# A planner's cost table: a longer way from the late loads to their use, and no delay between dependent passes on TensorE

## The chip, the cores and the metric

The kernel runs on one core of one Trainium2 chip. The metric is the device time of one execution in microseconds (us), median of several runs. Engines are named as in the profile: PE is TensorE (PEld its weight loads), DVE is VectorE, ACT is ScalarE, POOL is GpSimd, SP is SyncE, which issues nearly all DMAs.

## The reference, cut to what matters

Three layers follow each other: an attention over packed queries, a soft mixture of experts, and a feed-forward layer with a softmax gate and a norm. All inputs and the output are fp32.

```python
# attention: batch 8, heads 8, seq 576, head_dim 64, 32 packed queries p
p_packed = sm_attn(p, k, v); out = sm_attn(q, p_packed, p_packed)
# soft MoE: x (4608, 512), phi (512, 32), w1 (8, 512, 1024), w2 (8, 1024, 512), 4 slots an expert
logits = x @ phi
d = softmax(logits, axis=0); slot_input = d.T @ x
for e in range(8):
    slot_out[e] = maximum(slot_input[e] @ w1[e], 0) @ w2[e]
x = softmax(logits, axis=1) @ slot_out
# SoLU layer: w_in (512, 1024), w_out (1024, 512)
h = x @ w_in; solu = h * softmax(h)
out = ((solu - mean) / sqrt(var + 1e-6) * g_ln) @ w_out      # (4608, 512)
```

## The kernel before

The work has three phases. **Phase 1** is the attention and the logits, for four units `u` of two batches `b` each. The steps are named by their builders: `mk_A1` (scores of the packed queries against k), `mk_TR` (transposes), `mk_A4` (times v), `mk_BD`, `mk_B` (scores of q), `mk_S` (five groups `g` of transposes and a softmax a unit), `mk_A2T`, `mk_slots`. A(7) stands below for the step `mk_A` of batch 7, S(4,3) for group 4 of unit 3, the last step of `mk_S`. Phase 1 ends in `SIT`, the slots' input. **Phase 2** streams the experts' weights past `SIT`: `mk_w1` and `mk_w2` for experts 0 to 3, `mk_w1` for experts 4 to 7, and then the second weights of experts 4 to 7 (the late experts) in four column blocks k = 0 to 3 (`mk_block`), so that a block's result is ready for the next layer before the following block has arrived. When a block k is complete, ACT copies it (`so`, L1124), PE transposes it with a small matmul (`tr`, L1128), ACT writes it into `SO` (L1055), and PE multiplies it with the first weight of the last layer (`sw_pe`, L1330: two halves n of 512 columns for each block c; written sw(c,n) here). After sw(3,0) and sw(3,1), ACT and DVE write the two halves of `swr` (L1338, L1342). **Phase 3** needs `swr` for its first matmul (`h`, L1394) and then runs 36 tiles of 128 rows, bounded by the matmuls of L1533 and L1539.

The weights come as 256 *granules* of 128 KB, nine to a load `("w", i)` of 1152 KB. Load i is called w`i`. Granules 192 to 255 are those of the four blocks, 16 granules a block, four for each late expert; they lie in the loads w21 to w28. Load w27 is cut in three (1, 4 and 4 granules), and w28 has the last 4. One granule is 4 matmul records in the trace (two matmuls, each in two passes of fp32). SP issues all loads in one fixed order from one queue, each as soon as a buffer is free: 14 in `ring`, three more (`ring2`) for w5, w6 and w7, which lie over memory of phase 1. Of these, w6 waits for the last matmul of S(4,3), L556.

The order on every engine is made by a planner (`Plan`) when the kernel is built: each step is an `op` with a price in ns, its dependencies, and the buffers it takes and gives back; the delay from a step to one that depends on it comes from a table (`LAT`, 30 ns from PE to PE), from the step's own `lat` (2200 ns after a load) or from a pair `(step, delay)`. The planner walks through time, takes on each engine the ready step with the longest way to the end, repeats that 250 times with random changes to these ways, and keeps the order whose weighted goals come first (the last sw step 1.0, `SIT` 0.3, the last `wlo` 0.1). Where PE would idle in phase 1, a matmul on zeros fills it (L380), in one fixed place of the order. The planner also counts PE's matmuls, and prices the arrival of its next block of code:

```python
plan.blocks = (97, 126, 80, 3800, 45000)
plan.goals = [(x, 1.0), (o_SIT, 0.3), (o_lo, 0.1)]
```

The first block ends at matmul 97, each later one 126 further; a block is asked for 80 matmuls ahead and taken to need 3800 ns.

Of the kernel before, what the change touches and what calls it, by code (L numbers as in the profile page):

```python
# [179 lines left out]
def pack_attention__soft_moe__solu_kernel(  # L180
# [16 lines left out]
    NE = 8  # L197
# [21 lines left out]
    NS1, NS2, NS3 = 122, 125, 142  # L219
    NL = 4  # L220
    LATE = 32 * NE - 16 * NL
# [19 lines left out]
    with ExitStack() as p12, tc.manual_schedule():  # L241
# [18 lines left out]
        def op(*args, urgent=0, **kw):  # L260
            return plan.op(*args, urgent=urgent, rank=now[0], **kw)
# [30 lines left out]
        loaded, ld, W = {}, {}, {}  # L292

        def load(key, part):
            def go():
                if part == 0:
                    pool = W["ring2"] if key in RING2 else ring
                    loaded[key] = pool.tile([128, RW], FP32, tag="r", name="r")
                t = loaded[key]
                if key[0] in "kq":  # L300
                    c0, c1 = (1152 * c for c in halves(key)[part:part + 2])
                    nc.sync.dma_start(out=t[:, c0:c1], in_=(kT if key[0] == "k" else qT)[key[1]][:, c0:c1])
                elif key[0] == "v":
                    nc.sync.dma_start(out=t, in_=v[key[1], key[2]])
                elif key[0] == "w":
                    c0, c1 = (256 * c for c in cuts(key[1])[part:part + 2])
                    nc.sync.dma_start(out=t[:, c0:c1], in_=w12[key[1]][:, c0:c1])
                else:
                    src = (w_out if key[0] == "wo" else w_in)[key[1]].bitcast(UINT32)
                    nc.sync.dma_start(out=t[:, :2048].bitcast(UINT32), in_=src)  # L310

            return go
# [13 lines left out]
        def ring_of(key):  # L326
            return "ring2" if key in RING2 else "ring"

        o_pl = [p_load(0, 2)]
        for key in order:  # L330
            if key[0] in "kq":
                c = halves(key)
                ld[key] = [
                    op("DMA", 1425 * (c[n + 1] - c[n]), load(key, n), acq=[] if n else ["ring"], lat=2200)
                    for n in range(len(c) - 1)
                ]
            elif key[0] == "w":
                c = cuts(key[1])
                for part in range(len(c) - 1):
                    x = op("DMA", 317 * (c[part + 1] - c[part]), load(key, part), acq=[] if part else [ring_of(key)], lat=2200)  # L340
                    for j in range(c[part], c[part + 1]):
                        ld["g", 9 * key[1] + j] = x
            else:
                ns = 2540 if key[0] in ("wo", "wi") else 2850
                ld[key] = op("DMA", ns, load(key, 0), acq=[ring_of(key)], lat=2200)
            if key == ("v", 0, 0):
                o_pl.append(p_load(2, NB))
# [583 lines left out]
        y = op("DVE", 150, f0, [o_M[NU - 1], o_e], acq=["A2T"], rel=["A2T"])  # L931
        x = op("PE", 110, f1, [o_M[NU - 1], y], acq=["w"], pairs=1)
        x = op("DVE", 460, f2, [x, o_e], rel=["w"])
        x = op("PE", 110, f3, [x], acq=["w"], pairs=2)
        x = op("DVE", 70, f4, [x], rel=["w"])
        x = op("ACT", 190, f5, [x])
        x = op("DVE", 70, f6, [x, o_S[NU - 1]])
        x = op("PE", 110, f7, [x], acq=["w"], pairs=2)
        x = op("DVE", 736, f8, [x], rel=["w"])
        x = op("PE", 860, f9, [x, o_SI[NU - 1]], acq=["w"], pairs=8)  # L940
        x = o_SIT = op("DVE", 200, f10, [x], rel=["w"])
# [37 lines left out]
        o_hT, o_SOT, o_w1, o_w2, o_r2 = {}, {}, {}, {}, []  # L979
# [13 lines left out]
        def stream(g0, g1, pe, ns, deps, acq, rel):  # L993
            i = g0
            while i < g1:
                j = i + 1
                while j < g1 and ld["g", j] == ld["g", i]:
                    j += 1
                done = [ring_of(("w", i // 9))] if j % 9 == 0 or j == 32 * NE else []
                deps = [op("PE", ns * (j - i), pe(i, j), [ld["g", i]] + deps, acq=acq if i == g0 else [],  # L1000
                           rel=done + (rel if j == g1 else []))]
                if done == ["ring2"]:
                    o_r2.extend(deps)
                i = j
            return deps[0]

        def hz_zero():
            nc.gpsimd.memset(W["hz"], 0.0)
# [91 lines left out]
        def mk_block(k, e, dep):  # L1100
            s0 = LATE + 4 * (NL * k + e - NE + NL)

            def pe(g0, g1):
                def go():
                    if g0 == s0 and start:
                        ps_t["b", k] = bank()
                    for i in range(g0, g1):
                        for c in range(2):
                            q, r = divmod(i - s0, 2)
                            f = 2 * (i - s0) + c  # L1110
                            g, j = divmod(f, 2)
                            a = 2 * r + c
                            nc.tensor.matmul(
                                out=ps_t["b", k][32 * a:32 * a + 32, 0:128],
                                lhsT=hT_t[e][:, j, g, :],
                                rhs=gran(i)[:, 128 * c:128 * c + 128],
                                start=(start and q == 0),
                                stop=(end and q == 1),
                            )
                return go  # L1120

            def act():
                so_t["b", k] = W["k"].tile([128, 128], FP32, tag="so", name="so", bufs=3)
                nc.scalar.copy(so_t["b", k], ps_t.pop(("b", k))[:, 0:128])  # L1124

            def tr():
                ps_t["bt", k] = bank()
                nc.tensor.matmul(  # L1128
                    out=ps_t["bt", k][:, 0:4 * NL], lhsT=so_t["b", k], rhs=e4[:, 4 * (NE - NL):4 * NE], start=True, stop=True
                )  # L1130

            def act2():
                so_out(4 * (NE - NL), 4 * NE, k, k + 1, ps_t.pop(("bt", k))[:, None, 0:4 * NL])

            start, end = e == NE - NL, e == NE - 1
            y = stream(s0, s0 + 4, pe, NS3, [dep, o_hT[e], o_w2[NE - NL - 1]], ["w"] if start else [], [])
            if end:
                x = op("ACT", 200, act, [y], rel=["w"])
                x = op("PE", 165, tr, [x], acq=["w"])
                o_SOT["k", k] = op("ACT", 230, act2, [x], rel=["w"], urgent=10 ** 5)  # L1140
            return y
# [5 lines left out]
        x = None  # L1147
        for k in range(4):
            for e in range(NE - NL, NE):
                x = mk_block(k, e, x)  # L1150
# [13 lines left out]
        x = op("ACT", 1200, c_hi, [o_2], urgent=10 ** 5)  # L1164
        x = op("DVE", 1300, c_lo, [x], urgent=10 ** 5)
# [85 lines left out]
        o_wo, o_wi, o_bd = [], [], []  # L1251
# [47 lines left out]
        x = op("ACT", 480, sc_act, [o_bd[-1]], rel=["v"])  # L1299
        for f in (sc_dve, sc_dve2, sc_dve3, sc_dve4):  # L1300
            x = op("DVE", 430, f, [x], acq=["u"] if f is sc_dve2 else [])
        for k in range(8):
# [11 lines left out]
            y = op("DVE", 1300, q1, [x, o_wo[k]])  # L1314
            y = op("Pool", 700, q2, [y, o_3])
# [8 lines left out]
        def sw_pe(cs, ns):  # L1324
            def go():
                for n in ns:
                    if not cs[0]:
                        sw_t.append(W["ps"].tile([96, 512], FP32, tag="sw", name="sw"))
                    for c in cs:
                        nc.tensor.matmul(  # L1330
                            out=sw_t[n], lhsT=W["SO"][:, c].rearrange("p r s -> p (r s)"),
                            rhs=wif[:, c, 512 * n:512 * n + 512], start=(c == 0), stop=(c == 3),
                        )
            return go

        def mk_sw(n, dep):
            def act():
                nc.scalar.copy(W["sw"][n], sw_t[n])  # L1338

            def dve():  # L1340
                dst = W["sw"][n][64:96, :]
                nc.vector.tensor_tensor(out=dst, in0=sw_t[n][64:96], in1=dst.bitcast(FP32), op=ALU.subtract)  # L1342

            x = op("PE", 980, sw_pe((3,), (n,)), [dep, *o_SOT.values()])
            y = op("ACT", 478, act, [x], urgent=10 ** 6)
            op("DVE", 602, dve, [y], urgent=10 ** 6)
            return x

        x = None
        for c in range(3):  # L1350
            for n in range(2):
                x = op("PE", 980, sw_pe((c,), (n,)), [x, *o_wi, o_SOT["k", c]] + [o_SOT[e] for e in range(NE - NL)])
        x = mk_sw(0, x)
        x = mk_sw(1, x)
        plan.blocks = (97, 126, 80, 3800, 45000)
# [9 lines left out]
    with ExitStack() as p3, tc.manual_schedule():  # L1365
# [7 lines left out]
        op = plan.op  # L1373
# [326 lines left out]
```

## Time and profile before

| | us |
|---|---|
| median of 3 runs (lowest to highest) | 400.67 (400.15 to 402.09) |
| the profiled execution | 399.89 |
| its span, first to last instruction | 398.1 |
| phases 1 and 2, to the start of the first `h` | 182.0 |
| phase 3 | 216.1 |

The span is what the views below divide; the execution's own time has 1.8 us more around it. The profile gives busy time by engine, a strip of 40 slices, the chain of work that ended last, and for each wait which engine or DMA ended it.

### The profile page before, as it was taken

The numbers are of one execution on the slowest core, as the hardware profiler recorded it, in microseconds if no ns is written. First come the engines' busy times: TensorE is split into PE (matmuls) and PEld (weight loads), VectorE is DVE, ScalarE is ACT, GpSimd is POOL, SyncE is SP. The second block draws the span as 40 slices with busy tenths as digits, with TensorE's granted clock in tenths as the row PEclk, the third lists the DMA queues.
The fourth block names the chain that finished last, engine by engine and source line by source line (L and its number), as shares of the span: only waits on it lengthen the run. The fifth ranks groups of instructions, "written<-read, shape, count | busy, mean of one in ns | idle before, by whom it ended". The sixth has DMA issues, their size and how long they took to land.

```text
span 398.1 us, 9638 instructions
## 1 busy us (share of the span) xinstructions
PE 377.1 (95%) x3772; PEld 196.9 (49%) x3772; DVE 276.2 (69%) x562; ACT 231.3 (58%) x434; POOL 208.8 (52%) x311
## 2 busy tenths in 40 slices
PE   8889999988989998898999999999999999999996
PEld 3445566555535673543444444444444444444445
DVE  2169799888977838937977676676766776667621
ACT  1447797859544834105976665666556566755620
POOL 1033346334233572694878656556675666566630
PEclk9999999999999999999999999999999999999999
DMA  8999999999999999950267685677656655775771
GB/s 309 420 420 421 413 419 418 416 418 416 390 400 418 412 418 420 418 212 1 53 156 172 130 152 118 135 146 159 143 121 134 155 136 129 137 158 132 119 170 56
DMA packets 89421, 99.26 MB, mean 249 GB/s; under 512 B 75936, under 2 KB 76576, under 8 KB 82080
## 3 DMA queue, kind: packets, MB, share of 16 engines
q1 hardware_dynamic: 89088, 98.58, 75.9%
q8 instruction: 29, 0.48, 0.5%
q14 instruction: 16, 0.13, 0.1%
q10 hardware_dynamic: 288, 0.07, 0.1%
HBM read 70.85 MB, written 9.44 MB: 202 GB/s over the span
## 4 chain that ended last, share of the span: by engine, by line
PE 71%; DMA 15%; DVE 6%; ACT 3%; issue 2%; SPq 1%; POOL 0%; ACTq 0%; DVEq 0%; POOLq 0%
PE o L1533 29%; PE o L1539 14%; DMA r<-kT 6%; DMA r<-w 5%; PE h L1394 4%; PE sc L396 3%; PE w L1020 3%; DMA r<-qT 3%; PE w L1071 2%; PE w L556 2%; PE w L479 2%; PE sw L1330 2%; PE o L1546 1%; DVE s3t L1424 1%; PE w L670 1%
## 5 line engine op out<-in xcount | busy, mean ns | idle before, releaser
L1533 PE MATMUL o<-whi,th 128*128 128x512 f16 x280 | 106.2, 379 | 0.9 <-DMA th<-hi 0.9
L1533 PE MATMUL o<-wlo,th 128*128 128x512 f16 x280 | 106.1, 379 | 0.0
L1503 POOL TENSOR_TENSOR lo<-x,hi 128x1024 f16<-128x1024 f32 (+1 forms) x37 | 77.3, 2092 | 30.2 <-ACT hi L1481 28.5
L1533 PEld LDWEIGHTS <-th 128*128 128x128 f16 x560 | 54.6, 98 | 67.0 <-DMA th<-hi 1.4
L1539 PE MATMUL o<-whi,tl 128*128 128x512 f16 x280 | 66.5, 380 | 0.0
L1443 ACT ACTIVATE e<-s3t,nv 128x1024 f32<-128x1024 f32 x36 | 41.3, 1149 | 39.7 <-DVE nmean L1437 39.5
L1481 ACT ACTIVATE hi<-s3t,nr,rs 128x1024 f16<-128x1024 f32 x35 | 43.4, 1239 | 23.0 <-POOL nr L1464 22.8
L1424 DVE SCALAR_TENSOR_TENSOR s3t<-h,e 128x1024 f32<-128x1024 f32 (+1 forms) x37 | 44.0, 1190 | 17.3 <-ACT e L1415 17.2
L1402 DVE TENSOR_REDUCE nm<-h 128x1 f32<-128x1024 f32 (+1 forms) x37 | 44.0, 1191 | 14.0 <-PE h L1394 13.8
L1473 DVE TENSOR_SCALAR x<-s3t,nmean,rs 128x1024 f32<-128x1024 f32 x35 | 28.8, 824 | 23.1 <-POOL rs L1460 23.0
L1415 ACT ACTIVATE e<-h,nm 128x1024 f32<-128x1024 f32 (+1 forms) x37 | 39.9, 1079 | 7.5 <-DVE nm L1402 5.1
L1539 PEld LDWEIGHTS <-tl 128*128 128x128 f16 x280 | 24.9, 98 | 34.3 <-issue 8.6
L1394 PE MATMUL h<-swr,cT 96*128 96x512 f32 x72 | 28.9, 484 | 1.2 <-DVE swr L1342 0.9
L1561 DVE TENSOR_TENSOR ob<-o,winv 128x512 f32<-128x512 f32 x35 | 23.9, 684 | 7.2 <-PE o L1539 7.2
L380 PE MATMUL w<-wz 128*128 128x512 f16 x92 | 26.1, 379 | 0.8 <-DVE A L575 0.4
L600 POOL TENSOR_TENSOR A<-A,bsum 128x512 f32<-128x512 f32 (+1 forms) x18 | 18.1, 1020 | 15.8 <-DVE bsum L596 10.6
L1020 PE MATMUL w<-r,SIT 128*32 128x256 f32 x256 | 21.9, 384 | 0.0
L1460 POOL TENSOR_TENSOR rs<-rs,half 128x1 f32<-128x1 f32 x36 | 20.1, 558 | 2.9
L1459 POOL TENSOR_TENSOR rs<-V,w 128x1 f32<-128x1 f32 x36 | 7.4, 207 | 25.3 <-ACT e L1443 25.2
L454 POOL TENSOR_SCALAR r<-s 128x1 f32<-128x1 f32 x16 | 4.2, 265 | 30.2 <-ACT a L421 29.4
L421 ACT ACTIVATE a<-sc,nb 128x576 f32<-128x576 f32 x16 | 11.8, 739 | 13.6 <-DVE nb L416 13.5
L416 DVE TENSOR_REDUCE nb<-sc 128x1 f32<-128x576 f32 x16 | 11.5, 747 | 11.7 <-PE sc L396 11.7
(203 smaller groups left out, 635.6 us busy)
## 6 DMA issues: line engine op xcount, KB each, us to landing
r<-w SPq DMA_DIRECT2D x27, 1152.0 KB, 15.7
r<-v SPq DMA_DIRECT2D x8, 1152.0 KB, 21.5
r<-kT SPq DMA_DIRECT2D x7, 1152.0 KB, 22.0
r<-qT SPq DMA_DIRECT2D x7, 1152.0 KB, 22.2
out<-ob SPq DMA_DIRECT2D x31, 256.0 KB, 2.3
r<-w_in SPq DMA_DIRECT2D x4, 1024.0 KB, 22.0
r<-w_out SPq DMA_DIRECT2D x4, 1024.0 KB, 21.8
r<-w SPq DMA_DIRECT2D x3, 512.0 KB, 16.9
```

Of the source, the lines that this page charges most:

```text
L380: nc.tensor.matmul(out=t[:, 0:FN], lhsT=wz[:, 0:128], rhs=wz[:, 0:FN], start=True, stop=True)
L1020: nc.tensor.matmul(out=hp[32 * g:32 * g + 32, 0:256], lhsT=SIT[:, k, :], rhs=gran(i), start=(k == 0), stop=(k == 3),)
L1394: nc.tensor.matmul(out=w, lhsT=cT[:, t, :], rhs=swr[n], start=True, stop=True)
L1402: nc.vector.tensor_reduce(out=z["nm"][:, h:h + 1], in_=hcols(h), axis=AX.X, op=ALU.max, negate=True)
L1415: nc.scalar.activation(out=z["e"][:, cols(h)], in_=hcols(h), func=ACTF.Exp, bias=z["nm"][:, 0:1], accum_out=z["S"][:, h:h + 1],)
L1424: nc.vector.scalar_tensor_tensor(out=z["s"][:, cols(h)], in0=hcols(h), scalar=1.0, in1=z["e"][:, cols(h)], op0=ALU.mult, op1=ALU.mult, acc ...
L1443: nc.scalar.activation(out=z["e"], in_=z["s"], func=ACTF.Square, bias=z["nv"], scale=2.0 ** -15, accum_out=z["V"])
L1473: nc.vector.tensor_scalar(out=z["x"][:, cols(h)], in0=z["s"][:, cols(h)], scalar1=z["n"], scalar2=z["r"], op0=ALU.add, op1=ALU.mult,)
L1481: nc.scalar.activation(out=z["hi"][:, cols(h)], in_=z["s"][:, cols(h)], func=ACTF.Identity, scale=z["r"], bias=z["nr"])
L1503: nc.gpsimd.tensor_tensor(out=z["lo"][:, cols(h)], in0=z["x"][:, cols(h)], in1=z["hi"][:, cols(h)], op=ALU.subtract)
L1533: nc.tensor.matmul(out=z["o"], lhsT=z["th"][:, c, :], rhs=w[:, c, :], start=(c == 0 and w is whi), stop=False)
L1539: nc.tensor.matmul(out=z["o"], lhsT=z["tl"][:, c, :], rhs=whi[:, c, :], start=False, stop=(c == 7))
```

## The change

Three places of the planner's cost table change. A load w14 or later counts 2900 ns from its end to its first use, where it was 2200. Within a late expert's column blocks (granules from 192), a PE step that follows another of the same chain counts no delay, where it was 30 ns. The same holds between the sw steps. No operation, buffer, size or dependency changes; the planner's search runs again on the new prices.

```diff
-                    x = op("DMA", 317 * (c[part + 1] - c[part]), load(key, part), acq=[] if part else [ring_of(key)], lat=2200)
+                    x = op("DMA", 317 * (c[part + 1] - c[part]), load(key, part), acq=[] if part else [ring_of(key)],
+                           lat=2900 if key[1] >= 14 else 2200)
...
-                deps = [op("PE", ns * (j - i), pe(i, j), [ld["g", i]] + deps, acq=acq if i == g0 else [],
-                           rel=done + (rel if j == g1 else []))]
+                x = op("PE", ns * (j - i), pe(i, j), [ld["g", i]] + deps, acq=acq if i == g0 else [],
+                       rel=done + (rel if j == g1 else []))
+                deps = [(x, 0) if g0 >= LATE else x]
...
-            y = stream(s0, s0 + 4, pe, NS3, [dep, o_hT[e], o_w2[NE - NL - 1]], ["w"] if start else [], [])
+            y = stream(s0, s0 + 4, pe, NS3, [dep and (dep, 0), o_hT[e], o_w2[NE - NL - 1]], ["w"] if start else [], [])
...
-            x = op("PE", 980, sw_pe((3,), (n,)), [dep, *o_SOT.values()])
+            x = op("PE", 980, sw_pe((3,), (n,)), [(dep, 0), *o_SOT.values()])
...
-                x = op("PE", 980, sw_pe((c,), (n,)), [x, *o_wi, o_SOT["k", c]] + [o_SOT[e] for e in range(NE - NL)])
+                x = op("PE", 980, sw_pe((c,), (n,)), [x and (x, 0), *o_wi, o_SOT["k", c]] + [o_SOT[e] for e in range(NE - NL)])
```

The plan of phase 3 is word for word the same. SP's loads and stores stand in the same order. In phases 1 and 2 PE keeps its 214 steps, and 111 of them stand elsewhere, by up to 11 places; the zero fills that are emitted in phase 1 go from 92 to 82. Lines after 340 move by one, after 1000 by two.

PE, the end of phase 2, from the load w26 to the last sw step, before. `r_2900` is w26, `r_2945` w27, `r_2962` w28; `w_2920` is block 2, `w_2972` block 3; the rows with `so` are tr; `sw_2892` and `sw_2896` are the halves n = 0 and 1. Two matmuls are one granule.

```order
L1113 MATMUL w_2920<-r_2900,hz_2353 32x128 x12
L1113 MATMUL w_2972<-r_2900,hz_2353 32x128 x6
L1113 MATMUL w_2972<-r_2945,hz_2353 32x128 x2
L1128 MATMUL w_2984<-e4_61,so_2979 128x16
L1113 MATMUL w_2972<-r_2945,hz_2353 32x128 x8
L1330 MATMUL sw_2892<-wif_68,SO_2357 96x512
L1113 MATMUL w_2972<-r_2945,hz_2353 32x128 x8
L1330 MATMUL sw_2896<-wif_68,SO_2357 96x512
L1113 MATMUL w_2972<-r_2962,hz_2353 32x128 x8
L1128 MATMUL w_3018<-e4_61,so_3016 128x16
L1330 MATMUL sw_2892<-wif_68,SO_2357 96x512
L1330 MATMUL sw_2896<-wif_68,SO_2357 96x512
```

The same place after the change (`r_2876` is w26, `r_2908` w27, `r_2937` w28).

```order
L1115 MATMUL w_2896<-r_2876,hz_2333 32x128 x12
L1115 MATMUL w_2952<-r_2876,hz_2333 32x128 x6
L1115 MATMUL w_2952<-r_2908,hz_2333 32x128 x10
L1130 MATMUL w_2972<-e4_61,so_2959 128x16
L1115 MATMUL w_2952<-r_2908,hz_2333 32x128 x8
L1332 MATMUL sw_2872<-wif_68,SO_2337 96x512
L1115 MATMUL w_2952<-r_2937,hz_2333 32x128 x8
L1332 MATMUL sw_2900<-wif_68,SO_2337 96x512
L1130 MATMUL w_2998<-e4_61,so_2995 128x16
L1332 MATMUL sw_2872<-wif_68,SO_2337 96x512
L1332 MATMUL sw_2900<-wif_68,SO_2337 96x512
```

The last load's granules now stand ahead of sw(2,1), which stands between them and the last tr; each tr and sw(2,0) stand four granules further back.

PE, the loads w23 (`r_2824`) to w25 (`r_2877`), before; `w_2865` is block 1, `w_2920` block 2.

```order
L1113 MATMUL w_2865<-r_2824,hz_2353 32x128 x8
L1128 MATMUL w_2879<-e4_61,so_2874 128x16
L1113 MATMUL w_2865<-r_2824,hz_2353 32x128 x8
L1330 MATMUL sw_2892<-wif_68,SO_2357 96x512
L1330 MATMUL sw_2896<-wif_68,SO_2357 96x512
L1113 MATMUL w_2865<-r_2851,hz_2353 32x128 x16
L1113 MATMUL w_2920<-r_2851,hz_2353 32x128 x2
L1128 MATMUL w_2926<-e4_61,so_2924 128x16
L1113 MATMUL w_2920<-r_2877,hz_2353 32x128 x14
```

After (`r_2788` is w23, `r_2843` w25):

```order
L1115 MATMUL w_2847<-r_2788,hz_2333 32x128 x16
L1130 MATMUL w_2868<-e4_61,so_2856 128x16
L1332 MATMUL sw_2872<-wif_68,SO_2337 96x512
L1115 MATMUL w_2847<-r_2819,hz_2333 32x128 x16
L1115 MATMUL w_2896<-r_2819,hz_2333 32x128 x2
L1332 MATMUL sw_2900<-wif_68,SO_2337 96x512
L1130 MATMUL w_2906<-e4_61,so_2902 128x16
L1115 MATMUL w_2896<-r_2843,hz_2333 32x128 x18
```

The first tr has sw(0,0) right behind it, where four granules stood; sw(0,1) has moved behind the granules of w24.

PE, phase 1, from S(4,2) over A1(7) (the row with `p_sb`) to TR(7,0) before; rows with `wz` are zero fills, of which seven follow each other.

```order
L556 MATMUL w<-ident,ST 128x128 x6
L396 MATMUL sc<-r,p_sb 32x288 x16
L636 MATMUL w<-ident,A_1550 128x128 x4
L380 LDWEIGHTS wz
L380 MATMUL w<-wz 128x512
...
L439 MATMUL w<-ident,a 128x128 x4
L443 MATMUL w<-ident,a 128x128
L636 MATMUL w<-ident,A_1550 128x128 x4
```

After, from A1(7) on:

```order
L397 MATMUL sc<-r,p_sb 32x288 x16
L637 MATMUL w<-ident,A_1445 128x128 x4
L480 MATMUL w<-r,aT 32x64 x20
L381 LDWEIGHTS wz
L381 MATMUL w<-wz 128x512
L440 MATMUL w<-ident,a 128x128 x4
L444 MATMUL w<-ident,a 128x128
L504 MATMUL w<-ident,pb 128x128
L637 MATMUL w<-ident,A_1445 128x128 x4
```

A step A4 (L480) now stands between A1(7) and the transposes that wait for A1(7)'s softmax, and one fill is left of seven.

## Rows read from the trace of the kernel before

**Rows 1.** The page: busy time by engine, and GB/s moved in 40 slices.

```profile
PE 377.1 (95%) x3772; PEld 196.9 (49%) x3772; DVE 276.2 (69%) x562; ACT 231.3 (58%) x434; POOL 208.8 (52%) x311
...
GB/s 309 420 420 421 413 419 418 416 418 416 390 400 418 412 418 420 418 212 1 53 156 172 130 152 118 135 146 159 143 121 134 155 136 129 137 158 132 119 170 56
```

**Rows 2.** Busy time of the engines from 204 us on (start:end, length, PE first).

```profile
204.00:398.00 194.00, 190.79 (x900) 91.03 (x898) 124.91 (x220) 112.22 (x155) 116.30 (x191) 1.00 0.65 139
```

**Rows 3.** PE in order of time, 163 to 183 us: start, length, work, idle before.

```profile
163.88 0.85 PE L1113 MATMUL w<-r,hz 128*32 128x128 f32 x20 [1.38 <-DMA r<-w]
...
167.45 1.29 PE L1113 MATMUL w<-r,hz 128*32 128x128 f32 x36
...
169.47 1.07 PE L1113 MATMUL w<-r,hz 128*32 128x128 f32 x28 [0.17 <-DMA r<-w]
...
174.13 0.39 PE L1128 MATMUL w<-e,so 128*128 128x16 f32 x2
174.46 0.64 PE L1113 MATMUL w<-r,hz 128*32 128x128 f32 x16
175.03 1.10 PE L1330 MATMUL sw<-wif,SO 128*96 128x512 f32 x2
176.06 0.65 PE L1113 MATMUL w<-r,hz 128*32 128x128 f32 x16
...
177.67 0.65 PE L1113 MATMUL w<-r,hz 128*32 128x128 f32 x16
178.75 0.40 PE L1128 MATMUL w<-e,so 128*128 128x16 f32 x2 [0.44 <-ACT so L1124]
179.44 1.96 PE L1330 MATMUL sw<-wif,SO 128*96 128x512 f32 x4 [0.30 <-ACT SO L1055]
182.03 0.47 PE L1394 MATMUL h<-swr,cT 96*128 96x512 f32 x1 [0.63 <-DVE swr L1342]
```

**Rows 4.** The issue of single loads (w5, w6, w28), each with its landing.

```profile
L307 SPq DMA_DIRECT2D r<-w x1: 328/328/328, 95.4 to 95.4; - x1
...
DMA to landing us min/median/max: 16.6/16.6/16.6
...
L307 SPq DMA_DIRECT2D r<-w x1: 328/328/328, 108.9 to 108.9; - x1
...
DMA to landing us min/median/max: 5.9/5.9/5.9
...
L307 SPq DMA_DIRECT2D r<-w x1: 327/327/327, 161.1 to 161.1; - x1
...
DMA to landing us min/median/max: 15.3/15.3/15.3
```

**Rows 5.** The page's DMA issues: the run's first load, alone in its queue.

```profile
p_sb<-pT SPq DMA_DIRECT2D x1, 128.0 KB, 2.4
```

**Rows 6.** Windows behind the issue of w6, by microsecond; clock, DMA share, GB/s last.

```profile
108.00:109.00 1.00, 0.92 (x37) 0.52 (x35) 1.00 (x3) 0.89 (x2) 0.38 (x1) 1.00 0.65 255
109.00:110.00 1.00, 0.94 (x35) 0.57 (x17) 0.97 (x3) 0.27 (x1) 0.00 (x0) 1.00 0.77 230
110.00:111.00 1.00, 0.92 (x4) 0.35 (x4) 1.00 (x3) 0.96 (x4) 0.00 (x0) 1.00 0.81 267
```

**Rows 7.** PE in order of time, phase 1, 82 to 109 us.

```profile
82.52 1.73 PE L479 MATMUL w<-r,aT 128*32 128x64 f32 x80
...
88.47 0.72 PE L396 MATMUL sc<-r,p_sb 64*32 64x288 f32 x15 [1.61 <-issue]
...
89.61 1.68 PE L380 MATMUL w<-wz 128*128 128x512 f16 x7
92.00 0.66 PE L439 MATMUL w<-ident,a 128*128 128x128 f32 x4 [0.72 <-ACT a L421]
...
98.27 1.39 PE L479 MATMUL w<-r,aT 128*32 128x64 f32 x53 [0.92 <-issue]
...
108.36 0.44 PE L556 MATMUL w<-ident,ST 128*128 128x128 f32 x2
```

More of the change, by code (lines that the diff above doesn't have):

```diff
@@ L999, in stream @@
                 done = [ring_of(("w", i // 9))] if j % 9 == 0 or j == 32 * NE else []
-                deps = [op("PE", ns * (j - i), pe(i, j), [ld["g", i]] + deps, acq=acq if i == g0 else [],
-                           rel=done + (rel if j == g1 else []))]
+                x = op("PE", ns * (j - i), pe(i, j), [ld["g", i]] + deps, acq=acq if i == g0 else [],
+                       rel=done + (rel if j == g1 else []))
+                deps = [(x, 0) if g0 >= LATE else x]
                 if done == ["ring2"]:
-                    o_r2.extend(deps)
+                    o_r2.append(x)
                 i = j
-            return deps[0]
+            return x
         def hz_zero():
```

## The prediction

> **What bounds the kernel now.** I read the page first. PE is busy for 95% of the span, and yet PE isn't what limits the first part: the strip of GB/s stands near 418 from its second slice to its seventeenth, some 170 us (a slice is a fortieth of the span, 10 us), and then falls below 180 [rows 1]. So phases 1 and 2 run as fast as the weights arrive. Phase 3 is PE's: 190.8 of 194 us busy from 204 us on [rows 2]. Its plan is unchanged, so whatever the change does must show in the time at which the first `h` starts, 182.03 us [rows 3].
>
> Next I read PE's timeline at that border. Until w23 arrives PE is early: it idles 1.38 us for it at 163.88 and 0.17 us for w25 at 169.47 [rows 3]. From 169.47 on it is late: the last load, w28, lands at 161.1 + 15.3 = 176.4 us [rows 4], and PE takes its granules at 177.67, because sw steps and older granules stand ahead [rows 3]. After them PE idles 0.44 us until ACT has copied block 3 [rows 3]; tr starts at 178.75, PE idles another 0.30 us for `SO`, and sw(3,0) starts at 179.44 [rows 3]. The chain from there to `h` (sw, ACT, DVE, 2.59 us) doesn't move. Two things can therefore change the time: what PE does between w25 and sw(3,0), and when the loads land.
>
> **The end of phase 2, step by step.** Prices, all from one start to the next [rows 3]: four granules 0.57 us (174.46 to 175.03), nine 1.29 (the row of 36 records at 167.45), one sw step 1.03 (175.03 to 176.06), tr 0.33 (174.13 to 174.46), and 0.69 from the start of tr to the sw behind it when nothing stands between (178.75 to 179.44). I follow the new order with the old landings.
>
> - w23 at 163.88: nine granules, to 165.17. Then tr, with sw(0,0) right behind it: 165.17 + 0.69 = 165.86. Here some 0.3 us of idle is new, since four granules used to cover ACT's `SO`. sw(0,0) to 166.89, nine granules of w24 to 168.18, sw(0,1) to 169.21, tr to 169.54. The old order reached w25 at 169.47. Cost 0.07 us; the 0.17 us of waiting for w25 is its cover, and is used up.
> - w25: nine granules to 170.83, sw(1,0) and sw(1,1) to 172.89, nine granules of w26 to 174.18, one and four of w27 (0.14 + 0.57) to 174.89, tr to 175.22, four granules to 175.79, sw(2,0) to 176.82. All this work was there before too.
> - w28's four granules can start at 176.82. The load has landed by 176.4, so 0.42 us is left. They end at 177.39, and sw(2,1) runs to 178.42. This is the gain: the copy of block 3, for which PE idled, is now done under sw(2,1). From the last granule's end (177.67 + 0.57 = 178.24) to tr it was 0.51 us.
> - tr at 178.42, sw(3,0) at 179.11, where it was 179.44.
>
> That is **-0.3 us**. It can't be more with these landings. It falls to zero if w28 lands 0.42 + 0.3 us later against the rest. POOL's splitting of the last weight isn't waited for here: the first matmul that reads it is L1533, behind the whole chain of the first tile.
>
> **The moved order of phase 1.** This edit has no intended effect there, but the search ran again and phase 1 came out otherwise. Nearly all of its moves cost nothing as long as the loads keep flowing, and the loads depend on PE in one tight place: w6 waits for the last matmul of S(4,3), which starts at 108.36, and is issued at 108.9 [rows 4, 7]. The load ahead, w5, lands at 95.4 + 16.6 = 112.0 [rows 4]. How late may w6 be? The nearest row is the first load of the run, 128 KB in 2.4 us with nothing ahead [rows 5]. The other 1024 KB at 418 GB/s take 2.5 us, so w6 alone would need an estimated 4.9 us; it took 5.9 [rows 4]. S(4,3) may then come 1.0 us later for nothing, and costs 1 us for each us beyond. If it comes earlier, the most that can be won is the traffic lost around that issue: 255, 230 and 267 GB/s in the three windows from 108 to 111 us [rows 6] against 418: 163 + 188 + 151 = 502 KB too few, which take 1.2 us. The least is nothing, since w6 landed at 114.8, 2.8 us behind w5, the pace of 1152 KB (1.18 MB) at 418 GB/s: by this landing nothing was lost.
>
> So when does S(4,3) come? I price the two things that changed. First, the zero fills. Between A1(6) and S(4,3) the old order has 11, the new one 2; seven of the old ones stand in a row between A1(7) and TR(7,1), 1.68 us, and PE idles 0.72 us more before TR(7,1) [rows 7]. The new order puts an A4 step there (80 records of two of them took 1.73 us, 0.86 each [rows 7]). At 0.24 us a fill and with that idle time, up to 9 x 0.24 + 0.72 = 2.9 us earlier. Second, PE's idle time marked "issue": 1.61 us in A1(7), 0.92 us in A4(7,0) [rows 7]. Counted in the planner's way, these are the matmuls 1483 and 1609, where a block of PE's code ends. Both have some 80 fast records ahead; going back 80 from the first idle (17 of A1(7), 43 of `mk_slots`, S and BD, 20 of A4) leads into the row at 82.52, to about 83.8, and the next record is at 88.47, 4.7 us later. In the new order the ends from 1105 to 1609 fall into A4(5,0), A4(5,1), `mk_slots` of unit 1, A4(6,1) and A4(7,0): five places with fast records ahead, where the old order had two that idled. Three more idles of 0.92 to 1.61 us make 2.8 to 4.8 us; none make 0. The Trainium skill, in "Runtime: NRT & Kernel Launch", section "Instruction fetch mechanics", says that an engine's sequencer fetches its next 16 KiB page of 256 instructions by its own DMA queue while it runs the current one, and that crossing such a border costs little, "mostly hidden". By that rule the new borders cost nothing and S(4,3) comes 2.9 us early. The trace doesn't bear "hidden" out in this stretch: 1.61 and 0.92 us were in the open.
>
> The two nearly cancel: between 2.9 us early and 4.8 - 2.9 = 1.9 us late, without the fills' idle time won even 4.8 late. I take 0 to 0.5 us late, inside the 1.0 us that costs nothing. Term: **0**, bounds -1.2 and +1.9 - 1.0 = +0.9, at the worst +3.8.
>
> The loads behind w6 I leave out: `SIT`, on which the next ones wait, moves with S(4,3), and so do the landings ahead of them.
>
> **Sum.** 399.89 - 0.3 + 0 = 399.6 us for a profiled execution. The profiled one was 0.78 us under the median, so **400.4 us** as a median.
>
> **The rivals.**
>
> *The loads come earlier.* The fills' time is won and the code blocks cost little. For it: the idle of 2.4 us between A1(7) and TR(7,1) is real and is now used [rows 7]. Against it: only 1.2 us of traffic is there to win [rows 6], and w6's landing shows no gap. -0.3 - 1.2 gives 399.2 us. Chance 0.17. This is also where the Trainium skill's rule on instruction fetch would lead.
>
> *The loads come later (slower).* The place is w6 behind S(4,3), the price 1 us for each us beyond 1.0 [rows 4, 5], the mechanism one more "issue" idle of 1.6 us at each of three block ends [rows 7]. With three, S(4,3) is 1.9 to 4.8 us late and the sum +0.6 to +3.5: 401.3 to 404.2 us. It passes 0.5% when S(4,3) is 3.3 us late, that is after 111.7 us. Chance 0.18.
>
> *The end of phase 2 doesn't shorten.* w28 lands too late for its new place, or the new idle behind the first tr is longer than 0.3 us. Then 400.7 us. Chance 0.10.
>
> The forecast has the rest, 0.55.
>
> **How the numbers follow.** The measurement: the three runs spread from 400.15 to 402.09, so about 0.5%, 2 us, is what can be told from no change. The forecast and the last rival lie within it. Faster by over 0.5% (under 398.7) needs the first rival in full and a little more: 0.07. Slower by over 0.5% (over 402.7) is the upper half of the second rival, and a few executions: 0.12. The same: 0.81. The range of 8 in 10 reaches from the first rival's 399.2 to 402.4, where the second is two thirds through.
>
> **What would show it.** Right: in PE's timeline sw(2,1) stands between w28's granules and tr, no idle before tr, sw(3,0) 0.3 us earlier against w28's landing; some 0.3 us of idle between the first tr and sw(0,0); w28 lands at 176.4 give or take 1. Of the second term: L556's last matmul in phase 1 near 108.4, more "issue" idles on PE from 68 to 105 us and fewer fills. Wrong: w6 issued after 110 and every later landing shifted with it, or w6 issued before 107 and no sag of GB/s behind it with w28 a microsecond earlier. It would also be wrong if phase 3 changed its length of 216.1 us, which nothing in the change explains.

## The result, and the profile after

Four executions of the changed kernel took 404.38, 408.58, 410.99 and 412.01 us (median 409.78), four of the kernel before 400.15 to 402.26 (median 401.38). The ratio is 1.015 with an interval of 1.0111 to 1.0189: slower, clear of the noise, though by less than 2%. It leaves out two executions of after, 410.99 and 412.01 us, which lie over 1.5% above the fastest and show the lowest granted clock, 0.983. The profiled execution is the shortest of the four, 404.38 us with a span of 402.6; what follows explains its 4.5 us over the 399.89 of before.

The page's two strips of 40 slices, after (slices are 10 us):

```profile
PEclk9999999989999999999999999999999999999999
...
GB/s 318 416 420 416 418 418 421 416 419 416 355 258 424 349 419 418 420 357 4 26 107 189 165 144 120 141 139 162 121 130 157 132 140 122 158 147 128 122 169 63
```

Against [rows 1], GB/s sags in the eleventh and twelfth slices (390 and 400 before) and in the fourteenth (412 before), and the clock loses a tenth in the ninth. The ninth comes first. PE in order of time, 62 to 84 us, after; A1(5) is the row with `p_sb`, A4(5,0) and A4(5,1) are the rows of L480 at 71.74 and 78.25:

```profile
62.20 0.66 PE L557 MATMUL w<-ident,ST 128*128 128x128 f32 x4
62.78 0.91 PE L397 MATMUL sc<-r,p_sb 64*32 64x288 f32 x17
65.63 0.72 PE L397 MATMUL sc<-r,p_sb 64*32 64x288 f32 x15 [1.94 <-issue]
...
71.74 0.52 PE L480 MATMUL w<-r,aT 128*32 128x64 f32 x19
73.86 0.67 PE L480 MATMUL w<-r,aT 128*32 128x64 f32 x21 [1.60 <-issue]
...
78.25 0.62 PE L480 MATMUL w<-r,aT 128*32 128x64 f32 x31
80.98 0.61 PE L480 MATMUL w<-r,aT 128*32 128x64 f32 x9 [2.10 <-issue]
81.52 1.11 PE L557 MATMUL w<-ident,ST 128*128 128x128 f32 x4
```

Three short steps are cut in two by idles of 1.94, 1.60 and 2.10 us that nothing on another engine ended. They stand behind 979, 1105 and 1232 of PE's matmul records in the trace; counted as the planner counts (97 and 126 more each time), code blocks end at 979, 1105 and 1231. Before had two such idles, 1.61 and 0.92 us [rows 7]. The last line is the second effect: four transposes took 1.11 us, which take 0.66 at 62.20 in the first line. Windows behind the third idle, after (the clock is the third number from the end):

```profile
80.00:82.00 2.00, 1.02 (x12) 0.79 (x12) 0.56 (x3) 0.50 (x3) 0.00 (x0) 0.78 0.99 412
82.00:84.00 2.00, 2.00 (x11) 2.00 (x11) 1.36 (x3) 0.54 (x2) 0.00 (x0) 0.50 1.00 415
84.00:86.00 2.00, 2.00 (x27) 0.70 (x25) 1.62 (x7) 1.11 (x2) 0.00 (x0) 0.86 1.04 422
86.00:88.00 2.00, 2.00 (x57) 1.42 (x54) 1.84 (x4) 1.60 (x5) 1.05 (x1) 1.00 1.01 419
```

The granted clock falls to 0.50, the 1.2 GHz level, and is back at 1.00 before 86 us; by windows of one microsecond, the sum of 1 minus the clock is 1.71 us. Now the loads: SP at the issue of w6, after, and the windows behind it (GB/s last):

```profile
L307 SPq EVENT_SEMAPHORE  x1: 12677/12677/12677, 100.4 to 100.4; - x1
L307 SPq DMA_DIRECT2D r<-w x1: 327/327/327, 113.1 to 113.1; - x1
...
DMA to landing us min/median/max: 6.5/6.5/6.5
```

```profile
108.00:110.00 2.00, 1.88 (x48) 1.00 (x30) 2.00 (x8) 1.74 (x8) 0.00 (x0) 1.00 0.52 217
110.00:112.00 2.00, 2.00 (x28) 1.03 (x23) 1.97 (x7) 1.91 (x5) 0.96 (x1) 1.00 0.13 55
112.00:114.00 2.00, 1.61 (x16) 1.23 (x15) 1.93 (x7) 0.39 (x2) 0.77 (x2) 1.00 0.00 0
```

SP stands 12.7 us on one semaphore. S(4,3)'s last matmul comes at 112.66 us (108.36 before, [rows 7]), w6 is issued at 113.1 and lands at 119.6 (108.9 and 114.8, [rows 4]), and the DMA queues run empty, where [rows 6] had 230 GB/s at the least. The landings behind it are 4.2 to 6.5 us late: w28 lands at 166.5 + 15.3 = 181.8 us, 5.4 later than in [rows 4]. Not all of that comes through w6. Who SP waited for from 110 to 142 us (us in total, times, longest), after and then before:

```profile
SPq L307 <- PE w L1022: 21.1, 2, 17.1
SPq L307 <- PE w L557: 12.7, 1, 12.7
```

```profile
SPq L307 <- PE w L1020: 16.4, 2, 11.7
```

The longest of these waits, for the first weights' matmuls with `SIT` (L1022, L1020 before), is the one of w13: it is issued at 133.85 us and lands 5.1 us later than before, where w12 landed 4.2 later. The end of phase 2, after:

```profile
169.28 1.29 PE L1115 MATMUL w<-r,hz 128*32 128x128 f32 x36 [1.51 <-DMA r<-w]
170.49 0.39 PE L1130 MATMUL w<-e,so 128*128 128x16 f32 x2
171.19 1.10 PE L1332 MATMUL sw<-wif,SO 128*96 128x512 f32 x2 [0.30 <-ACT SO L1057]
...
182.23 0.64 PE L1115 MATMUL w<-r,hz 128*32 128x128 f32 x16
182.80 1.10 PE L1332 MATMUL sw<-wif,SO 128*96 128x512 f32 x2
183.74 0.29 PE L1130 MATMUL w<-e,so 128*128 128x16 f32 x2
184.33 1.96 PE L1332 MATMUL sw<-wif,SO 128*96 128x512 f32 x4 [0.30 <-ACT SO L1057]
186.92 0.47 PE L1396 MATMUL h<-swr,cT 96*128 96x512 f32 x1 [0.63 <-DVE swr L1344]
```

It runs as the prediction walked it: 0.30 us of new idle behind the first tr, none before the last tr. From w28's landing (181.84 to two places) to sw(3,0) it is 2.49 us, where it was 3.04 [rows 3, 4]. So: 5.44 us from the landings, less 0.55 at the end of phase 2, less 0.4 in phase 3 (402.6 - 186.92 = 215.7 us, 216.1 before) makes the 4.5. Phase 3 took 215.3 to 216.4 us in the fourteen profiles of this document, so those 0.4 us are within its spread.

### The profile page after: what moved, and what is told of

Its sections match the earlier page's. It is cut to its first block, busy times and chain, and to the rows that moved or that the text cites. A ratio compares the mean times of both kernels' runs of the same rounds, so it can differ in the third digit from the quotient of the medians.

```text
span 402.6 us, 9621 instructions
## 1 busy us (share of the span) xinstructions
PE 376.1 (93%) x3762; PEld 197.6 (49%) x3762; DVE 276.0 (69%) x562; ACT 231.6 (58%) x434; POOL 209.2 (52%) x311
## 4 chain that ended last, share of the span: by engine, by line
PE 67%; DMA 15%; DVE 9%; ACT 4%; issue 3%; SPq 0%; POOL 0%; ACTq 0%; POOLq 0%
PE o L1535 28%; PE o L1541 14%; DMA r<-w 8%; DMA r<-kT 5%; PE h L1396 4%; PE sc L397 3%; PE w L1022 3%; PE w L480 2%; DMA r<-v 2%; PE o L1548 1%; DVE bmx L569 1%; DVE bsum L589 1%; DVE s3t L1426 1%; PE w L381 1%; PE w L557 1%
## 5 line engine op out<-in xcount | busy, mean ns | idle before, releaser
L381 PE MATMUL w<-wz 128*128 128x512 f16 x82 | 23.6, 380 | 1.8 <-ACT A2T L645 0.6
L1022 PE MATMUL w<-r,SIT 128*32 128x256 f32 x256 | 21.6, 383 | 0.0
```

What stands on the lines that cost most here:

```text
L381: nc.tensor.matmul(out=t[:, 0:FN], lhsT=wz[:, 0:128], rhs=wz[:, 0:FN], start=True, stop=True)
L1022: nc.tensor.matmul(out=hp[32 * g:32 * g + 32, 0:256], lhsT=SIT[:, k, :], rhs=gran(i), start=(k == 0), stop=(k == 3),)
```

## The experiments

Theory A: the new order of phase 1 lets blocks of PE's code end where short matmuls stand in a row; PE idles, the clock falls behind the idles, phase 1 ends late, and the loads that wait for it come late. Theory B: the new order or prices of phase 2 cost it. Theory C: the clock falls by itself. In all runs with a fixed order, the search's result is replaced by a written list of the steps:

```diff
+FIXED = [
...
+]
...
+def _fixed(self):
...
+    for i in FIXED:
+        self.ops[i][2]()
+Plan.run = _fixed
```

**All results in one table.** "Idle" is the sum of PE's idles marked issue from 5 to 125 us, "clock" the sum of 1 minus the granted clock over windows of 1 us there, both in us of the profiled execution; w13 and w28 are landings; the ratio is to the kernel before, measured beside it.

| | idle | clock | w13 | w28 | profiled | ratio (interval) |
|---|---|---|---|---|---|---|
| before | 2.96 | 0 | 135.0 | 176.4 | 399.89 | |
| after | 6.30 | 1.71 | 140.1 | 181.8 | 404.38 | 1.015 (1.0111 to 1.0189) |
| e1_p1old_p2new | 3.89 | 0 | 135.7 | 177.3 | 400.18 | 0.9987 (0.9971 to 1.0002) |
| e2_p1new_p2old | 9.07 | 3.40 | 143.9 | 186.3 | 410.31 | 1.0223 (1.0176 to 1.027) |
| e3_shift35 | 12.24 | 5.13 | 147.9 | 189.2 | 411.97 | 1.0234 (1.0192 to 1.0276) |
| e4_ring2_moved | 10.42 | 6.82 | 147.3 | 188.3 | 410.86 | 1.022 (1.0192 to 1.0247) |
| e5_lat_only | 9.14 | 5.13 | 146.3 | 186.8 | 409.47 | 1.0244 (1.0192 to 1.0297) |
| e6_delay_only | 2.65 | 0 | 135.0 | 176.7 | 400.2 | 0.9989 (0.9967 to 1.0011) |
| e7_shift35 | 0.37 | 0 | 135.0 | 177.1 | 399.57 | 0.9982 (0.9958 to 1.0005) |
| e8_before_shift25 | 2.73 | 0 | 134.7 | 176.1 | 399.08 | 0.9992 (0.9972 to 1.0012) |
| e9_shift10 | 6.00 | 1.71 | 139.1 | 181.2 | 405.52 | 1.0144 (1.0112 to 1.0177) |
| e10_before_shift70 | 2.84 | 1.71 | 137.0 | 178.7 | 401.09 | 1.0006 (0.9988 to 1.0024) |
| e11_after_seed2 | 6.12 | 1.71 | 139.6 | 180.4 | 402.96 | 1.001 (0.9974 to 1.0045) |
| e12_price5400 | 1.73 | 1.71 | 135.3 | 177.9 | 400.58 | 1.0003 (0.9989 to 1.0016) |

**Which half of the program.** Two lists: before's order up to PE's first step of the experts and after's from there on, and the converse.

> The order of before up to PE's first step of the experts, from there on the order of after. Theory A (the moved order of phase 1 lets blocks of PE's code end in fast runs of small matmuls, PE idles, S(4,3) and with it w6 come late): S(4,3) ends its last matmul near 108.4 us, w6 is issued near 108.9, w28 lands near 176.4, and only the shorter end of phase 2 is left of the change: 0.3 to 0.6 us under the kernel before in its own runs, ratio 0.998 to 1.000. Theory B (the moved order of the weights' steps in phase 2 holds back a load's buffer): w6 early as before, but w28 lands 4 to 5.5 us late all the same, ratio 1.010 to 1.019. Theory C (the granted clock falls in this program for a reason that has nothing to do with the idles): no telling where, but the clock is under 0.99 of the span in most executions.

> The converse: the order of after up to PE's first step of the experts, from there on that of before. Theory A: as slow as after and 0.3 to 0.6 us slower, for the end of phase 2 has its old order: three idles of 1.6 to 2.1 us marked issue between 65 and 84 us, w6 issued near 113, w28 landing near 182, ratio 1.010 to 1.020. Theory B: within 0.3% of before. Theory C: the clock falls where it fell in after only if the idles are there.

With before's phase 1 the loss is gone, as theory A expected, and 2.47 us from w28's landing to sw(3,0) show the gain at the end of phase 2. With after's phase 1 the loss is there, but beyond theory A's numbers: the ratio is 1.0223 where 1.020 was the most, and w28 lands at 186.3. Only two of the three idles were as long as expected (the one in A4(5,1) was 0.47 us), two more blocks idle (1.58 and 2.86 us in A4 steps at 95.91 and 105.12), and the clock falls twice. Theory B falls.

**Which of the edits.** Each alone, the search free:

```diff
-                           ... lat=2200)
+                           lat=2900 if key[1] >= 14 else 2200)
```

> Only the longer way of the loads from w14 on. PE's rows of phase 1 come out word for word those of after; the end of phase 2 does not get after's order of the last load. Theory A (where the blocks of PE's code end in phase 1 decides, with the granted clock that falls behind the idles): as slow as after, ratio 1.010 to 1.024, idles of 1.6 us and more at the same matmuls of A1(5) and A4(5,0) as in after, w13 issued 4 us or more after 128.6, w28 landing 4 us or more after 176.4. Theory B (the new prices hurt in phase 2): slow as well only if the reordering of phase 2 that this edit brings does it, with w6 issued before 110.

> Only the delays of nothing. PE's rows of phase 1 come out word for word those of before; sw(2,1) stands behind w28's granules, as in after. Theory A: no loss, and what the end of phase 2 gives: ratio 0.997 to 1.000, 0.3 to 0.6 us under before in the profiled runs, w6 issued at 108.5 to 109.5. Theory B with the delays as the culprit: ratio over 1.010.

The loads' longer way alone brings the whole loss, with 1.94 and 1.60 us at the same places of A1(5) and A4(5,0); the delays of nothing bring the end of phase 2 (2.50 us from w28 to sw(3,0)) and no loss. Whether that end makes the kernel faster can't be told: the ratio is 0.9989, its interval holds 1, and the profiled execution was not under before's as expected (400.2 against 399.89 us). A price for loads that land after 130 us made phase 1 slow, through the search alone.

**Whether the place of the blocks' ends does it.** No step is moved; small matmuls behind one zero fill push the ends.

```diff
+                def go(kk=k):
...
+                        for _ in range(35 if kk == 23 else 0):
+                            nc.tensor.matmul(out=t[0:32, 0:16], lhsT=wz[:, 0:32], rhs=wz[:, 0:16], start=True, stop=True)
```

The first try (`if k == 23`) read the loop's variable after the loop had ended, so that no small matmul was in the program:

> The order of after without a step moved, and 35 matmuls of 16 columns on zeros right behind the last zero fill ahead of A1(1), where PE waits 1.2 us for a load. They do nothing but push every later end of a code block 35 matmuls forward in the work. Theory A: the ends of 979, 1105 and 1231 fall elsewhere, the three idles of 1.94, 1.60 and 2.10 us shrink (by counts on after's own durations to about 1.0, 0.4 and 1.0), the clock stays at 1.00 around 82 us, S(4,3) comes 3 to 5 us sooner than in after, at 107.5 to 109.5, w28 lands at 176 to 178, ratio 0.998 to 1.004. Theory B: w28 lands 4 us late or more, ratio 1.010 to 1.019. Theory C: the clock falls all the same, ratio over 1.006.

It is therefore a second profile of after's instructions, and its 408.5 to 411.97 us belong to the same order. The same instructions idled at more places than in the first profile, 2.04 us at 38.11 and 2.86 us at 110.15 among them, and the clock fell behind three of the idles, not one. With the matmuls in:

> What the run e3_shift35 was meant to be: the order of after without a step moved, and 35 matmuls of 16 columns on zeros behind the last zero fill ahead of A1(1), now in the program. Theory A: every later end of a code block falls 35 matmuls earlier in the work; the idles marked issue between 25 and 112 us come to 5 us or less (6.3 to 12.2 in the four profiled executions of this order so far), the clock falls at most once, S(4,3) ends at 106 to 110 us, ratio 0.998 to 1.006. If the order itself is at fault and not where its code blocks end: ratio 1.010 to 1.024 as before.

> As e7_shift35, but 10 small matmuls in place of 35: the control for whether small matmuls as such help. By going 80 records back from every block's end in the trace of e7_shift35, and taking 4.9 us from the asking to the arrival, the idles of phase 1 come to 16.5 us with 10 and 18.8 with none, against 5.6 with 35 (an estimate that does not see waits for data, so too high in all three). Theory A: slow like after, ratio 1.008 to 1.024, with idles of 5 us or more in sum and the clock falling at least once. If the small matmuls help by themselves, or by the wait that they fill: ratio 0.997 to 1.003.

PE with 35 small matmuls: A1(5), a wait for POOL, A4(5,0), A4(5,1) and, in the last line, S(4,3):

```profile
20.87 1.03 PE L383 MATMUL w<-wz 128*32 128x16 f16 x35
...
63.59 1.20 PE L399 MATMUL sc<-r,p_sb 64*32 64x288 f32 x32
...
67.70 0.66 PE L639 MATMUL w<-ident,A 128*128 128x128 f32 x4 [1.34 <-POOL A L603]
...
71.55 0.90 PE L482 MATMUL w<-r,aT 128*32 128x64 f32 x40
...
76.63 1.05 PE L482 MATMUL w<-r,aT 128*32 128x64 f32 x36
77.61 0.66 PE L559 MATMUL w<-ident,ST 128*128 128x128 f32 x4
...
107.34 0.38 PE L559 MATMUL w<-ident,ST 128*128 128x128 f32 x2
```

With 10 of them:

```profile
65.90 1.18 PE L399 MATMUL sc<-r,p_sb 64*32 64x288 f32 x25 [2.14 <-issue]
...
74.80 1.06 PE L482 MATMUL w<-r,aT 128*32 128x64 f32 x31 [1.98 <-issue]
75.78 1.12 PE L639 MATMUL w<-ident,A 128*128 128x128 f32 x4
...
82.55 0.66 PE L482 MATMUL w<-r,aT 128*32 128x64 f32 x19 [1.23 <-issue]
```

35 matmuls that compute nothing take the loss of 8 to 10 us away (median 399.68 us). With 10 the kernel is still 5.5 us slower than before (405.78 against 400.29), and its idles stand at the same three steps, ten records earlier in each (x25, x31 and x19 behind the idle, where after has x15, x21 and x9). This is the test that settles it: same steps, same order, same prices, other ends. The control isn't clean, for 10 matmuls gave back part of the loss; that small matmuls help by their number is made unlikely by the idles, which moved by exactly ten records, and by the next run, where 25 of them made the kernel before no faster (ratio 0.9992).

Theory C has no run of its own, since none held the clock. With 35 matmuls the profiled execution shows no fall of it in phase 1, but the ten executions' mean clocks reach from 1.000 down to 0.987, and the four lowest (0.987 and three of 0.991) belong to the four longest times (402.75 and 400.52 to 401.39 us). So the clock still fell in some, without bringing the loss of after back; what it fell behind there isn't shown.

The same in the order of before:

> The converse on the kernel before: its own order, no step moved, and 25 such small matmuls in the same place, which by counts on its own steps move two more ends of blocks into fast runs (steps A1(5), A4(5,0) and A4(7,0): 2.0, 1.7 and 3.2 us, where it has 0.9, 0.5 and 1.8 by the same count). Theory A: slower than before with no other edit: idles marked issue of 5 to 9 us in sum (2.96 in before), the clock falls behind one of 2 us, w6 issued 1.5 to 6 us later, ratio 1.003 to 1.015. If the ends of code blocks do not matter: ratio 0.998 to 1.002, for the 25 matmuls lie in a wait of 1.2 us for a load.

> As e8_before_shift25, which moved the ends to places that turned out harmless, but with 70: by the same count on that run's trace 16.1 us, against 11.0 with none and 10.8 with 25. The matmuls themselves cost PE at most 0.7 us beyond the wait that they lie in. Theory A: slower than before though no step has moved, idles of 5 us or more in sum, the clock falls behind those of 2 us, ratio 1.004 to 1.020. If the order of before is safe whatever its ends: 0.998 to 1.003.

Theory A's expectation was missed in both. With 25 one end idles over 0.4 us, 1.95 us in a step of S, where the order had 1.61 and 0.92 us without them. With 70 two do, 1.82 us at 41.05, with the clock at half behind it, and 0.59 at 88.15; w28 lands 2.3 us later in that profile, but the median is 400.53 us against 400.29. The count, 80 records back and 4.8 us on, overrates the idles, and none of the three ends that it named for 25 matmuls idled. That before becomes slow by other block ends alone is therefore not shown; these two shifts didn't do it.

**Whether w6 is the only tight place.** The second ring takes other loads.

```diff
-    RING2 = (("w", 5), ("w", 6), ("w", 7))
+    RING2 = (("w", 9), ("w", 10), ("w", 11))
```

> The order of after; the second ring takes w9, w10 and w11 in place of w5, w6 and w7, which go into the ring of 14, so that no load waits for S(4,3) before w10. The step that opens the memory of the last phase stands somewhat later in the order, ahead of its first use. The idles of PE stay. Theory A says that they cost only through w6: the three idles and the fall of the clock are still seen, S(4,3) is as late as in after (112 to 113 us), but the strip of GB/s shows no hole at 110 to 114 us, w28 lands at 176 to 178, ratio 0.996 to 1.003. If the late phase 1 costs in another way as well (SIT, on which every step of the experts waits), w28 is late all the same and the ratio stays over 1.008.

The strip of GB/s, and the issue of w13 (released by a step of L1022, the first weights' matmuls with `SIT`):

```profile
GB/s 314 420 419 414 417 419 422 419 418 418 350 419 326 34 404 421 421 409 105 1 103 179 159 128 154 128 138 138 137 155 131 132 131 149 156 131 123 134 164 68
...
L307 SPq DMA_DIRECT2D r<-w x1: 328/328/328, 140.9 to 140.9; - x1
...
DMA to landing us min/median/max: 6.4/6.4/6.4
```

w6 lands at 115.7 us though S(4,3) comes only at 119.66, so its wait can be removed; but the hole moves to 132 to 141 us and nothing is won. The expectation's second case holds: the end of phase 1 bounds the loads twice, at w6 and again at w13. Before, w13 too was issued with little to spare: at 128.61 us, landing at 134.97, 2.80 behind w12.

**Whether the prices are at fault.** The search from another seed, and a dearer code block:

```diff
-        rnd = random.Random(1)
+        rnd = random.Random(2)
```

```diff
-        plan.blocks = (97, 126, 80, 3800, 45000)
+        plan.blocks = (97, 126, 80, 5400, 45000)
```

> The changed prices, the search started from another random seed: another phase 1, the block's arrival still priced at 3800 ns. By counts on the steps of the plan its ends come to 6.8 us of idles, where after came to 11.8 and before to 7.0. Theory A: the prices did not make the kernel slow, this draw of the search did: ratio 0.996 to 1.006, w6 issued at 107 to 110. If the changed prices are at fault whatever the draw: 1.010 or more.

> The changed kernel with a code block's arrival priced at 5400 ns in place of 3800, nearer to the 4.6 to 5.5 us seen between asking and resuming in the traces. The count on its steps gives 5.2 us of idles, the least of the plans looked at. Theory A: idles marked issue of 4 us or less in sum, no fall of the clock, ratio 0.995 to 1.002. If the price of a block does not reach what happens on the chip: anywhere from 1.000 to 1.020, with idles that the plan did not see.

With the changed prices in place, neither shows after's loss as a whole. The second seed keeps part of it: its profile has one idle of 2.56 us at 100.69, w6 issued at 111.2 where 107 to 110 was expected, and w28 landing 4.0 us late, and five of its ten executions took 402.0 to 402.96 us, the other five 398.6 to 401.11. The dearer block kept within 399.53 to 401.04 us. Its details were partly missed: the idles came to 1.73 us as expected, but the clock did fall, at 111 us, behind a stretch in which PE waited 0.77 us for ACT and not for its code. One draw each doesn't tell whether the price of 5400 ns or another order did it. Neither beats the kernel before by more than can be told.

## Why the prediction was wrong

The forecast of 400.4 us and the range up to 402.4 failed; the rival *the loads come later* happened, beyond its price (401.3 to 404.2 us), and with its sign: w6 was issued after 110, and the landings behind it were late. Two of the prediction's readings don't follow from its own numbers: 402.4 lies little over a third of the way from 401.3 to 404.2, not two thirds, and the rival's 1.9 to 4.8 us of lateness count three idles of 1.61 us, while three of 0.92 with the fills won would be 0.1 us early.

**The term of phase 1, taken as 0, is the step that failed.** Its first half, the fills: up to 2.9 us were to be won. With hardly an idle left at a block's end (e7_shift35), S(4,3) starts its last matmuls only 1.0 us before the 108.36 of [rows 7] (107.34 us), though it has 2.6 us less of such idles than before. So next to nothing of the fills' 2.9 us was won: PE waits for DVE, ACT and POOL in other places (1.34 us for POOL's `A` at 67.70 in that run). Its second half: three more idles of 0.92 to 1.61 us, 2.8 to 4.8 in sum, or none. In the profile of after they were three of 1.60 to 2.10 us in place of before's two; all idles marked issue made 3.34 us more than before, so this half was right in size. In other executions of this phase 1 there were five to eight. Of the five ends that I had called places "with fast records ahead", two idled in the profile of after (those in A4(5,0) and A4(5,1)); the one in A1(5), 1.94 us, wasn't among the five. I then let these idles cancel against a gain that had one row for it.

**The clock was left out.** No term of the sum holds a fall of the granted clock, since before shows 1.00 throughout phase 1. By the table's measure it took 1.71 us in the profile of after and 3.4 to 6.8 us in four others of its phase 1.

**That 1.0 us of lateness costs nothing was wrong.** S(4,3) came 4.3 us later and w6 landed 4.8 later, where the rule gave 3.3; in e10, w6 was issued 2.2 us later than in before and landed 2.05 later. w28 came 5.4 later in after. By the prediction's rule the sum would have been 399.89 - 0.3 + 3.3 = 402.9 us; it was 404.38. The rule also knew only of w6, and "the loads behind w6 I leave out" was a term put at nothing: w13, which waits for the first steps with `SIT`, is a second place with the same price, as e4_ring2_moved showed. What the runs put in its place is a sum made after the fact: w13 lands later than before by about the idles beyond 2.96 us plus the clock's loss. After: 3.34 + 1.71 = 5.05, measured 5.1; e2: 9.5, 8.9; e5: 11.3, 11.3; e9: 4.75, 4.1; e10: 1.6, 2.0; e11: 4.9, 4.6; e3 and e4, the two longest, fit less well: 14.4 and 14.3 by the sum, 12.9 and 12.3 measured. Downward there is nothing to win, as the prediction said: e7 has 2.6 us less of idles, and w13 lands where it did.

**The end of phase 2 was right in its mechanism and too small in size:** 0.55 us for the predicted 0.3, and 0.54 to 0.57 in the runs e1 and e6, which have it without the loss. So "it can't be more" was wrong: sw(2,1) took 0.94 us to the start of tr where 1.03 was the price, and from tr to sw(3,0) it was 0.59 for 0.69. These 0.2 us more are below what the executions' times can tell.

**Why PE idles there.** The trace shows one packet of 16,384 bytes on a queue of its own for each block (29 packets, 0.48 MB in the page's list; PE's 3762 records make 29 blocks behind the first 97). The queues of after between 63.1 and 64.4 us:

```profile
q1 hardware_dynamic: 61, 0.50, 95.1%
q8 instruction: 1, 0.02, 5.3%
```

That packet runs from 63.20 to 64.31 us; PE's last record before the idle starts at 63.29, and PE goes on at 65.63, 1.32 us behind the packet. The other two idles of after end 1.20 and 1.28 us behind theirs (71.56 to 72.66, 78.61 to 79.70), and all 46 idles of this kind over 0.4 us between 20 and 125 us in the fourteen profiles end 1.2 to 1.6 us behind a packet. The Trainium skill ("Runtime: NRT & Kernel Launch", "Instruction fetch mechanics") says that pages of 16 KiB come by a queue of their own, and the packets agree; "mostly hidden" holds in phase 3, where no profile has such an idle over 0.15 us, and for most blocks of phase 1, but not for 5.64 us of after's. What sets the moment at which a packet starts stays open: at the three idles of after it started with 1, 19 and 2 records left before the block's end, at all its other blocks with 42 or more, and the planner's rule of 80 records does not tell these apart. Open too is why the same instructions idle at three places in one execution and at eight in another, and how much of a loss the clock alone makes, since no run held the clock.

## What to carry to other kernels

A change of a cost table is a new draw of the whole order, also where its prices don't apply: look at the new ends of code blocks in every stretch of short matmuls, not only at the place that was meant. Where an order is slow by its block ends, a few matmuls that do nothing, in a wait that is there anyway, can give the time back (35 did here, 10 only in part); another seed did in half of its executions, and a dearer block in all ten, which one draw each can't tell from luck. And two estimates of 3 us that cancel are not a term of zero: the range has to hold both.

## What the runs showed of the hardware

Code blocks that come late cost PE up to 2.9 us at a place (2.86 at 105.12 in e2_p1new_p2old), and the clock can double it: 1.60 us at 73.81 in that run were followed by a fall of 1.71 by the table's measure. Behind such an idle the granted clock stood at 0.50 for 2 to 3 whole microseconds, once for five (e5_lat_only, 106 to 111 us) and once for six (e4_ring2_moved, 108 to 114 us). It did not do so behind every one: 1.94 us at 65.63 in after left the clock at 1.00, 1.60 us at 73.81 in e2_p1new_p2old did not; and in e12_price5400 it fell with no late block just before it. The eight executions of after's instructions (after and e3_shift35) lie between 404.4 and 412.0 us, the 67 of the kernel before between 399.2 and 404.6.
